# A Hyena filter and a cosine-gated MLP on one core: transformed data made the stationary operand of the last step, x turned in blocks by VectorE, and places of 129 elements

## The chip, the cores and the metric

The kernel runs on one core of a Trainium2 chip. The metric is the device time of one launch in microseconds. All arithmetic is float32. In the profile PE is TensorE's matmuls, PEld its weight loads, DVE is VectorE, ACT ScalarE, POOL GpSimd, SP SyncE, which issues every DMA of this kernel.

## What is computed

```python
# x, v: (4, 12480, 128); pos_emb: (12480, 64); w1: (64, 64); w2: (64, 128)
h_filt = (np.maximum(pos_emb @ w1, 0.0) @ w2) * np.exp(-0.01 * pos)[:, None]
u = x * v
L = 2 * S
y = np.fft.irfft(np.fft.rfft(u, n=L, axis=1) * np.fft.rfft(h_filt, n=L, axis=0)[None], n=L, axis=1)[:, :S]
a = (x * y).reshape(B * S, D)
# moe_w_in: (128, 2048), moe_w_out: (2048, 128)
h = a @ w_in
out = (h * np.cos(h)) @ w_out
```

A long causal convolution over 12,480 positions in each of 128 channels, multiplied by x, and then a feed-forward layer on each of the 49,920 rows. (The float64 weights of the second part are turned into float32 on the chip.)

## The kernel before

**The transform.** The convolution is a Fourier transform of length N1 x N2 = 96 x 120, done by matmuls in two steps each way. A sequence position is n1 x 120 + n2, with n1 up to R = 104. The steps of one batch, by the names of the functions that issue them:

- u: x and v are loaded with n1 on the partitions, multiplied (L395), and the sums and differences of positions that mirror each other are written to the big buffer `slots` (L401).
- f1 (`f1_mm`, L407): the transform over n1. For each channel a 104 x 124 slice of `slots` (n1 by place) is the stationary operand, loaded as weights, and the table c1 (192 columns) streams. `f1_evict` (L415 to L425) writes the result back over the same channel.
- f2 (`f2_mm`, L448): the transform over n2. A table w (124 x 120) is stationary, and all 128 channels of one place, real and imaginary, stream: 256 columns. `f2_product` (L467 to L474) multiplies by the filter's transform h, on DVE and POOL.
- i1 (`i1_mm`, L479): back over k2. For each channel a 120 x 96 slice of `slots` is stationary and the table cs (120 columns) streams. `i1_evict` (L487, L489) writes sums and differences.
- i2 (`i2_mm`, L504): back over k1. A table tm (96 x 104) is stationary and all channels of one place stream (128 columns). The output has n1 on the partitions; `i2_out` (L511) multiplies it by x, loaded the same way (xs), and stores a group of four n2 (`n2s`) to zd in HBM.

A float32 matmul appears in the profile as two instructions, each with its own weight load.

**The layout of slots.** It is `[P, CB, 2*N2, 2]`: 64 pairs of channels, then 240 places, then the two channels of the pair. A slice of one channel over the places steps by two elements; all channels of one place are 64 pairs, 480 elements apart. `parts`, `above`, `aT` and `ftile` are views or tiles of the same kind.

**The feed-forward part.** 98 tiles of up to 128 rows of four n2, so up to 512 columns. `moe_load` (L727) brings a tile zb from zd; `moe_turn` transposes it with four TensorE transposes (L126) into PSUM, and ACT copies it to `at` (L737). For each of 16 chunks of 128 hidden units: `moe_up` (L743, then ACT L746, DVE L749, POOL L752), `moe_act` (ACT L757, DVE L759) and, four steps later, `moe_down` (L768). `moe_back` transposes the result again with TensorE and `moe_store` writes it.

**The order.** It is written out by hand. First the setup: the filter's network, f1 of the filter, f1 of batch 0 (beside the conversion of the first weights), f2 of both together (`f2_both_units`, which keeps h in hd and w in wd), i1 of batch 0 (beside the conversion of the second weights and some tables). `cs` is loaded just before f2 of both, into a pool of its own. From then on the main loop goes through 98 x 16 steps of the feed-forward part and, between them, advances the convolution of the batches by generators: each yields how many steps its piece counts for (I1_STEPS 0.8 a channel pair, I2_STEPS 1.5 a group, and so on), and `owed` keeps the balance. `load(n)` first advances the convolution until the rows of tile n are made. A tile is loaded at step 12 of the tile two before it, and turned at step 3 of the tile before it. `units` gives each kind of piece its pattern: `before` (loads, some pieces ahead), `mm` (matmuls), `after` (what follows the matmuls, one piece late).

Of the kernel before, what the change touches and what calls it, by code (L numbers as in the profile page):

```python
# [30 lines left out]
def kernel(  # L31
# [74 lines left out]
    LAG = 4  # L106
    WCOL = 256

    dram = ctx.enter_context(tc.tile_pool(name="dram", bufs=1, space=DRAM))
    hd = dram.tile([N1 // 2, N2, 2, CB, 4], F32, name="hd")  # L110
    zd = dram.tile([NROWS, G, D], F32, name="zd")
# [241 lines left out]
    def filter_out(pool, bank, aT, slots, j, w2_sb):  # L353

        ps = bank()
        for i, jj in enumerate((j, H - 1 - j)):
            nc.tensor.matmul(ps[0:FR, i * 2 * D:(i + 1) * 2 * D], aT[:, jj, 0:FR],
                             w2_sb[:, :], start=True, stop=True)
        above = pool.tile([FR, 2, CB, 2], F32, name="above", bufs=2)
        pj = ps[0:FR, :].rearrange("p (n b i) -> p n b i", n=4, i=2)  # L360
        nc.scalar.copy(out=above[:, :, :, :], in_=pj[:, 2:4])
        a = H - 2 - 2 * j
        for place, op in ((a, ALU.add), (ODD + a, ALU.subtract)):
            nc.vector.tensor_tensor(
                slots[0:FR, :, place:place + 2, :].transpose([0, 2, 1, 3]),
                pj[:, 1::-1], above[:, :, :, :], op=op)
# [14 lines left out]
    def clear_gap(u):  # L381

        nc.gpsimd.memset(u[:, :, H:ODD, :], 0.0)
# [13 lines left out]
    def u_sums(u, tiles, a):  # L397
        both = tiles[0][:, :, :].rearrange("p h (n b i) -> p h n b i", n=UA, i=2)
        below, above = both[:, 0, ::-1, :, :], both[:, 1, :, :, :]
        for place, op, e in ((a, ALU.add, nc.gpsimd), (ODD + a, ALU.subtract, nc.vector)):  # L400
            e.tensor_tensor(u[0:R, :, place:place + UA, :].transpose([0, 2, 1, 3]),  # L401
                            below, above, op=op)


    def f1_mm(ps, u, b, i):

        nc.tensor.matmul(ps[0:KE, i * 2 * N1:(i + 1) * 2 * N1], u[:, b, 0:KE, i],  # L407
                         c1[0:u.shape[0], :, :].rearrange("p r k -> p (r k)"),
                         start=True, stop=True)
# [10 lines left out]
    def f1_evict(ps, b, share):  # L420
        copy, negated = f1_takers(b, share)
        pj = ps[:, 0:4 * N1].rearrange("p (i r k) -> p r k i", i=2, r=2)
        copy(out=parts[0:ODD, :, :, b, :], in_=pj[0:ODD])
        yield
        copy(out=parts[ODD:KE, 0, :, b, :], in_=pj[ODD:KE, 1])  # L425
        negated(parts[ODD:KE, 1, :, b, :], pj[ODD:KE, 0])
        yield

    def f1_evict_filter(ps, b, share):

        copy, negated = f1_takers(b, share)
        pj = ps[:, 0:4 * N1].rearrange("p (i k) -> p k i", i=2)
        near, far = ftile[:, b, :, :], above[:, b, :, :]
        copy(out=near[0:ODD], in_=pj[0:ODD, 0:N1 + KF])
        copy(out=far[0:ODD], in_=pj[0:ODD, N1 + KF:])
        yield
        copy(out=near[ODD:KE, 0:N1], in_=pj[ODD:KE, N1:])
        negated(near[ODD:KE, N1:], pj[ODD:KE, 0:KF])
        negated(far[ODD:KE], pj[ODD:KE, KF:N1])
        yield  # L440

    def f2_mm(ps, w, k1, i, filt=False):
# [3 lines left out]
        pi = ps[0:N2, :].rearrange("p (r b g i) -> p g r b i", r=2, g=2, i=2)[:, i]  # L446
        if not filt:
            nc.tensor.matmul(pi, w[:, i, :], parts[0:KE, :, k], start=True, stop=True)  # L448
        elif k < KF:
            both = ftile[0:KE, :, k:k + N1 + 1:N1, :].rearrange("p b r i -> p r b i")  # L450
            nc.tensor.matmul(pi, w[:, i, :], both, start=True, stop=True)
        else:
            for r, src in enumerate((ftile[0:KE, :, k, :], above[0:KE, :, k - KF, :])):
                nc.tensor.matmul(pi[:, r], w[:, i, :], src, start=True, stop=True)

    def f2_product(pool, ps, h, k1, whole):


        y = parts[0:N2, :, k1:k1 + 2, :, :].rearrange("p r k b i -> p r b (k i)")
        t = pool.tile([N2, 2, CB, 4], F32, name="t", bufs=1 + whole)  # L460
        uu = ps[0:N2, :].rearrange("p (r b j) -> p r b j", r=2, j=4)
# [15 lines left out]
    def i1_mm(ps, b, i):  # L477
        for r in range(2):
            nc.tensor.matmul(  # L479
                ps[0:N1, (i * 2 + r) * N2:(i * 2 + r + 1) * N2],  # L480
                parts[0:N2, r, :, b, i],
                cs[:, r, :], start=True, stop=True)

    def i1_evict(pool, ps, b):
# [3 lines left out]
        for h, op in ((0, ALU.add), (1, ALU.subtract)):  # L488
            nc.vector.tensor_tensor(slots[0:N1, b, h * N2:(h + 1) * N2, :], pj[:, 0],  # L489
                                    other[:, :, :], op=op)  # L490
            yield

    def i2_mm(ps, t, g, part):
        for i in range(part * G // 2, (part + 1) * G // 2):
# [8 lines left out]
            for r, place in enumerate(places):  # L503
                nc.tensor.matmul(ps[0:R, i * D:(i + 1) * D], t[:, i, r, :],  # L504
                                 slots[0:N1, :, place, :], start=(r == 0), stop=(r == 1))

    def i2_out(pool, ps, xs, b, g):
        if b == 0:
            yield
        zs = pool.tile([R, 2, UA, D], F32, name="zs")  # L510
        nc.vector.tensor_tensor(  # L511
            zs[:, :, :, :].rearrange("p h n d -> p (h n d)"), ps[0:R, :],
            xs[:, :, :].rearrange("p h n -> p (h n)"), op=ALU.mult)
        z = zs[:, :, :, :].rearrange("p h n d -> p (h n) d")
        row = (b * NG + g) * R
        if row > 0:
            nc.sync.dma_start(zd[row:row + R, :, :], z)
        else:
            zbs[0] = z
        made[0] += 1  # L520
        yield

    rows_psum = []
    made = [0]
    zbs = {}
# [65 lines left out]
    def f2_units(bank):  # L591
        with tc.tile_pool(name="there", bufs=3) as pool:
            ws, hs = {}, {}

            def before(j):
                ws[j] = pool.tile([KE, 2, N2], F32, name="w")
                nc.sync.dma_start(ws[j][:, :, :], wd[j, :, :, :])
                hs[j] = pool.tile([N2, 2, CB, 4], F32, name="h")
# [11 lines left out]
    def f2_both_units(bank):  # L610

        with tc.tile_pool(name="both", bufs=2) as pool:
# [15 lines left out]
            def after(j, ps):  # L628
                h = pool.tile([N2, 2, CB, 4], F32, name="h", bufs=3)
                nc.scalar.activation(h[:, :, :, :].rearrange("p r b j -> p (r b j)"),  # L630
# [34 lines left out]
    def i2_units(bank, b, bufs):  # L665

        with tc.tile_pool(name="back", bufs=2, side="left" if b else "right") as pool:
            ts, xss = {}, {}

            def before(j):  # L670
                ts[j] = pool.tile([N1, G, 2, R], F32, name="tm", bufs=bufs)
                xss[j] = pool.tile([R, 2, UA * D], F32, name="xs", bufs=bufs)
                load_pairs(xss[j], x, b, n2s(j)[0], n2s(j)[UA])
                if b == 0 and j not in SOME:
                    return make_group(pool, j, ts[j], 1)
                nc.sync.dma_start(ts[j][:, :, :, :], td[j, :, :, :, :])

            def mm(j, ps, i):
                if i == 0:
                    ps = bank()  # L680
                i2_mm(ps, ts[j], j, i)
# [3 lines left out]
                             lambda j, ps: i2_out(pool, ps, xss.pop(j), b, j),  # L685
                             4 if b == 0 else 2, ahead=bufs - 1, skip=int(b == 0))

    def inverse_units(bank, b):
# [6 lines left out]
        new = u_units(b + 1, 3, slots[0:R, :, :, :],  # L695
# [10 lines left out]
    def forward_units(bank, back):  # L706

        f2 = f2_units(bank)
        next(f2)
        yield from f1_units(bank, slots[0:R, :, :, :])  # L710
# [13 lines left out]
    def moe_load(pool, n):  # L724
        m, row = rows_of(n), first_row(n)
        zb = pool.tile([P, G, D], F32, name="zb", bufs=2)
        nc.sync.dma_start(zb[0:m, :, :], zd[row:row + m, :, :])  # L727
        zbs[n] = zb

    def moe_turn(pool, n):  # L730
        m = rows_of(n)
        zb = zbs.pop(n)
        pt = ps_h.tile([P, BANK], F32, name="ph")
        for i in range(G):
            transpose(pt[:, i * m:(i + 1) * m], zb[0:m, i, :], ident)
        at = pool.tile([D, BANK], F32, name="at")
        nc.scalar.copy(out=at[:, 0:G * m], in_=pt[:, 0:G * m])  # L737
# [62 lines left out]
    with tc.manual_schedule():  # L800
        with tc.tile_pool(name="psum", bufs=8, space=PSUM) as psum, \
# [5 lines left out]
            slots = spool.tile([P, CB, 2 * N2, 2], F32, name="slots")  # L807
            parts = slots[:, :, 0:2 * N1, :].rearrange("p b (r k) i -> p r k b i", r=2)
            above = slots[:, :, 2 * N1:2 * N2, :]
            aT = above.rearrange("p b j i -> p b (j i)")  # L810
# [5 lines left out]
            with tc.tile_pool(name="layers", bufs=1, side="right") as pool:  # L816
# [10 lines left out]
                first_u = u_units(0, 3, slots[0:R, :, :, :],  # L827
# [24 lines left out]
            ftile = fpool.tile([P, CB, N1 + KF, 2], F32, name="ftile")  # L852
            clear_gap(ftile[0:FR, :, :, :])
            with tc.tile_pool(name="out", bufs=1, side="right") as pool:
                for j in range(H // 2):
                    filter_out(pool, bank, aT, ftile, j, w2_sb)
                    for _ in range(1 + (j % 3 == 0)):
                        next(first_u)
            f1 = f1_units(bank, ftile[0:FR, :, :, :], 0.53, f1_evict_filter)
# [15 lines left out]

            def beside(units, pieces, more=lambda pool: iter(())):
                with tc.tile_pool(name="convert", bufs=1) as pool:
                    convert, other = convert_units(pool, pieces), more(pool)
                    for i, _ in enumerate(units):
                        if i % 14 == 0:  # L880
# [6 lines left out]
            beside(f1_units(bank, slots[0:R, :, :, :], 0.55),  # L887
                   [(wind[:, c], w) for c, w in in_pieces])
            lpool = ctx.enter_context(tc.tile_pool(name="late", bufs=1))
            cs = third_table(lpool)  # L890
            nc.sync.dma_start(cs[:, :, :], csd[:, :, :])
            for _ in f2_both_units(bank):
# [3 lines left out]
            wpool = ctx.enter_context(tc.tile_pool(name="weights", bufs=1))  # L896
            rows, tw_t = last_tables(wpool)
# [22 lines left out]
        mpool = ctx.enter_context(tc.tile_pool(name="moe", bufs=2))  # L920

# [4 lines left out]
        def convolutions():  # L926
            for b in range(B):
# [5 lines left out]
                if b + 1 < B:  # L933
                    yield from forward_units(bank, backs[b + 1])
# [11 lines left out]
        moe_turn(mpool, 0)  # L946
        steps = [(n, c) for n in range(NALL) for c in range(NFC)]
        hidden, gates, ots, obs = {}, {}, {}, {}
        for i in range(len(steps) + LAG):
            if i < len(steps):  # L950
                n, c = steps[i]
                if n == 0 and c == NFC // 2:
                    load(1)
                if c == NFC - 4 and n + 2 < NALL:
                    load(n + 2)
# [8 lines left out]
            if i < len(steps):  # L964

                if c == (LAG - 1 if n else NFC - 2) and n + 1 < NALL:
                    moe_turn(mpool, n + 1)
# [37 lines left out]
```

## Time and profile before

| what | value |
|---|---|
| time, three runs | 3759.83, 3760.59, 3761.09 us (median 3760.59) |
| span of the profiled execution | 3758.9 us, 47,177 instructions |
| setup, up to the first product of the feed-forward part | 343.9 us |
| f1 of batches 1, 2, 3 (first to last matmul) | 594 to 729, 1410 to 1541, 2233 to 2364 us |
| f2 of batches 1, 2, 3 | 734 to 1021, 1549 to 1835, 2371 to 2658 us |
| i1 of batches 1, 2, 3 | 1031 to 1172, 1843 to 1986, 2665 to 2809 us |
| i2 of batches 0 to 3 | 338 to 565, 1178 to 1383, 1992 to 2206, 2815 to 2946 us |
| feed-forward part alone | 2946 us to the end |
| DMA | 209,499 packets, 276.14 MB, 73 GB/s on average |

The time of a run is that of the launch; the profiled execution is known by its span, which starts with its first instruction and ends with its last. In a group of instructions the columns are line, engine, operation, tiles, shape and number; busy time and mean duration of one in ns; and the engine's idle time before them with what ended it. A matmul's duration is longer than its share of the stream, since matmuls are pipelined: the distance from start to start is what counts.

### The profile page before, as it was taken

The page shows a single profiled execution, that of the slowest core. Times are in us where ns is not written, and L with a number is a line of the kernel's source. Part 1 is how long each engine was busy: PE and PEld are TensorE (multiplying, and loading weights), DVE is VectorE, ACT ScalarE, POOL GpSimd, SP SyncE. Part 2 cuts the span into 40 slices and gives each one's busy share as a digit, 9 for nine tenths or more (in the row PEclk, how much of TensorE's full clock was granted, in tenths as well). Part 3 has the DMA queues.
Part 4 walks back from the last instruction along what each step waited for, and adds up shares of the span by engine and source line. Part 5 has one row for each costly group of instructions (what it writes and reads, how often), then busy time and mean ns, then how long its engine had stood idle before and what let it go on. Part 6 is the DMA issues. An engine that isn't in the chain of part 4 may idle for free.

```text
span 3758.9 us, 47177 instructions
## 1 busy us (share of the span) xinstructions
PE 3690.6 (98%) x13546; PEld 2110.4 (56%) x13546; DVE 2773.7 (74%) x5586; ACT 2508.2 (67%) x4660; POOL 2557.6 (68%) x2318
## 2 busy tenths in 40 slices
PE   7898999999999999999999999999999999999999
PEld 6777555555566556555565556555566544444444
DVE  8887997687866787788766776788765666666666
ACT  5757776766665557766665567666664677777777
POOL 6666776588845665688745664788644677777776
PEclk9999999999999999999999999999999999999999
DMA  6263551022203650122104530122105200000000
GB/s 167 64 185 107 155 167 33 25 72 79 72 12 91 181 151 12 40 79 77 52 18 128 180 105 21 52 79 76 38 21 172 76 23 17 17 23 18 17 23 13
DMA packets 209499, 276.14 MB, mean 73 GB/s; under 512 B 17111, under 2 KB 146535, under 8 KB 209111
## 3 DMA queue, kind: packets, MB, share of 16 engines
q1 hardware_dynamic: 209239, 273.12, 24.8%
q8 instruction: 109, 1.79, 0.2%
q14 instruction: 151, 1.24, 0.1%
HBM read 193.64 MB, written 79.42 MB: 73 GB/s over the span
## 4 chain that ended last, share of the span: by engine, by line
PE 88%; DVE 3%; POOL 3%; ACT 2%; DMA 2%; issue 1%; SPq 0%; POOLq 0%; DVEq 0%; ACTq 0%
PE ph L743 33%; PE acc L768 28%; PE cv L504 5%; PE cv L768 5%; PE cv L479 4%; PE cv L407 3%; PE cv L448 3%; PE ph L126 2%; POOL f L752 1%; PE ps L407 1%; PE ps L448 1%; DMA tm<-td 1%; DMA wd<-w 1%; ACT cs L757 1%; DVE k L749 1%
## 5 line engine op out<-in xcount | busy, mean ns | idle before, releaser
L752 POOL TENSOR_TENSOR f<-a,k 128x512 f32<-128x512 f32 (+1 forms) x1568 | 1986.2, 1267 | 1060.5 <-DVE k L749 1059.1
L743 PE MATMUL ph<-at,w_in_sb 128*128 128x512 f32 (+1 forms) x3136 | 1599.0, 591 | 3.7 <-DVE gt L759 2.7
L746 ACT ACTIVATE a<-ph,quarter 128x512 f32<-128x512 f32 (+1 forms) x1568 | 1071.2, 683 | 704.8 <-PE ph L743 695.2
L768 PE MATMUL acc<-gt,w_out_sb 128*128 128x512 f32 (+1 forms) x2688 | 1370.3, 591 | 0.0
L759 DVE TENSOR_TENSOR gt<-ph,cs 128x512 f32<-128x512 f32 (+1 forms) x1568 | 1077.3, 687 | 359.9 <-ACT cs L757 341.8
L757 ACT ACTIVATE cs<-f 128x512 f32<-128x512 f32 (+1 forms) x1568 | 981.0, 626 | 366.6 <-POOL f L752 364.3
L749 DVE TENSOR_SCALAR k<-a 128x512 f32<-128x512 f32 (+1 forms) x1568 | 792.9, 506 | 550.7 <-ACT a L746 524.2
L768 PEld LDWEIGHTS acc<-gt,w_out_sb 128*128 128x128 f32 x2688 | 508.4, 189 | 642.8 <-issue 631.9
L743 PEld LDWEIGHTS ph<-at,w_in_sb 128*128 128x128 f32 x3136 | 553.2, 190 | 337.7 <-issue 257.5
L474 POOL TENSOR_TENSOR slots<-slots,t 120x256 f32<-120x256 f32 x384 | 312.9, 821 | 59.9 <-DVE t L467 25.6
L504 PEld LDWEIGHTS cv<-slots,tm 96*104 96x104 f32 x1920 | 238.6, 169 | 106.8 <-issue 85.4
L504 PE MATMUL cv<-slots,tm 96*104 96x128 f32 x1920 | 251.7, 273 | 9.9 <-POOL tm L297 5.0
L768 PE MATMUL cv<-gt,w_out_sb 128*128 128x512 f32 (+1 forms) x448 | 224.5, 583 | 1.0 <-DVE gt L759 1.0
L479 PEld LDWEIGHTS cv<-cs,slots 120*96 120x96 f32 x1536 | 176.7, 167 | 67.2 <-issue 65.2
L479 PE MATMUL cv<-cs,slots 120*96 120x120 f32 x1536 | 183.2, 266 | 0.0
L448 PEld LDWEIGHTS cv<-slots,w 124*120 124x120 f32 x576 | 103.7, 184 | 124.3 <-issue 112.3
L407 PEld LDWEIGHTS cv<-c,slots 104*124 104x124 f32 x768 | 132.6, 192 | 72.2 <-issue 60.0
L448 PE MATMUL cv<-slots,w 124*120 124x256 f32 x576 | 173.0, 380 | 0.0
L407 PE MATMUL cv<-c,slots 104*124 104x192 f32 x768 | 151.8, 327 | 5.4 <-DVE gt L759 3.5
L768 PEld LDWEIGHTS cv<-gt,w_out_sb 128*128 128x128 f32 x448 | 84.9, 190 | 104.8 <-issue 99.5
L489 DVE TENSOR_TENSOR slots<-cv,other 96x240 f32<-96x240 f32 x384 | 133.1, 394 | 1.5 <-ACT other L487 1.4
L395 DVE TENSOR_TENSOR xt<-xt,vt 104x256 f32<-104x256 f32 x177 | 132.6, 751 | 0.6 <-DMA vt<-in_v_dram 0.6
(131 smaller groups left out, 2520.9 us busy)
## 6 DMA issues: line engine op xcount, KB each, us to landing
h<-hd SPq DMA_DIRECT2D x144, 240.0 KB
tm<-td SPq DMA_DIRECT2D x96, 312.0 KB
xt<-in_x_dram SPq DMA_DIRECT2D x120, 208.0 KB
vt<-in_v_dram SPq DMA_DIRECT2D x120, 208.0 KB
xs<-in_x_dram SPq DMA_DIRECT2D x120, 208.0 KB
zd<-zs SPq DMA_DIRECT2D x119, 208.0 KB
zb<-zd SPq DMA_DIRECT2D x96, 256.0 KB
w<-wd SPq DMA_DIRECT2D x144, 116.2 KB
```

The lines of the kernel that those rows point to most:

```text
L407: nc.tensor.matmul(ps[0:KE, i * 2 * N1:(i + 1) * 2 * N1], u[:, b, 0:KE, i], c1[0:u.shape[0], :, :].rearrange("p r k -> p (r k)"), start=Tr ...
L448: nc.tensor.matmul(pi, w[:, i, :], parts[0:KE, :, k], start=True, stop=True)
L474: nc.gpsimd.tensor_tensor(y[:, r], y[:, r], t[:, r], op=op)
L479: nc.tensor.matmul(ps[0:N1, (i * 2 + r) * N2:(i * 2 + r + 1) * N2], parts[0:N2, r, :, b, i], cs[:, r, :], start=True, stop=True)
L504: nc.tensor.matmul(ps[0:R, i * D:(i + 1) * D], t[:, i, r, :], slots[0:N1, :, place, :], start=(r == 0), stop=(r == 1))
L743: nc.tensor.matmul(ph[:, 0:m], w_in_sb[:, c * P:(c + 1) * P], ats[n][:, 0:m], start=True, stop=True)
L746: nc.scalar.activation(a[:, 0:m], ph[:, 0:m], AF.Identity, bias=quarter[:, 0:1], scale=INV_TWO_PI)
L749: nc.vector.tensor_scalar(out=k[:, 0:m], in0=a[:, 0:m], scalar1=ROUND, scalar2=ROUND, op0=ALU.add, op1=ALU.subtract)
L752: nc.gpsimd.tensor_tensor(f[:, 0:m], a[:, 0:m], k[:, 0:m], op=ALU.subtract)
L757: nc.scalar.activation(cs[:, 0:m], f[:, 0:m], AF.Sin, scale=TWO_PI)
L759: nc.vector.tensor_tensor(gt[:, 0:m], ph[:, 0:m], cs[:, 0:m], op=ALU.mult)
L768: nc.tensor.matmul(accs[n][:, 0:m], w_out_sb[:, c, :], gt[:, 0:m], start=(c == 0), stop=(c == NFC - 1))
```

## The change

- `slots` becomes `[P, 2*N2, 129]`: a place is 129 elements, 128 channels in a row and one unused. All channels of one place are now contiguous; a slice of one channel steps by 129 elements (516 bytes). `parts`, `above`, `ftile` and hd follow. `filter_out` takes two unused stretches of `slots` for its temporary.
- In i2 the operands change places: the 128 channels of one place are loaded as weights and the table's 104 columns stream. The output has the channels on the partitions and n1 in the columns, as the feed-forward part needs it.
- `moe_turn` is gone: `moe_load` loads `at` from zd, which now has the channels first, in two or three pieces of up to 104 rows. A tile is loaded at step 8 of the tile before it. The first tile is made in `at` itself.
- x must now be turned for the multiplication. For each batch, 64 DMAs copy x from HBM to HBM into blocks (`blocks_units`); they are issued during f1, one every second piece, for batch 0 during its f1 and f2. For each group four DMAs load 32 partitions each (`blocks_load`), and VectorE transposes 32 x 32 blocks (`blocks_turn`) right after the product of the group before.
- `cs` is loaded after f2 of both, with the other tables.

```diff
-    zd = dram.tile([NROWS, G, D], F32, name="zd")
+    xd = dram.tile([B, H, D // SQ, UA, ROWB, NB, SQ], F32, name="xd")
+    zd = dram.tile([B * NG, D, G, R], F32, name="zd")
...
-        nc.tensor.matmul(ps[0:KE, i * 2 * N1:(i + 1) * 2 * N1], u[:, b, 0:KE, i],
+        nc.tensor.matmul(ps[0:KE, i * 2 * N1:(i + 1) * 2 * N1], u[:, 0:KE, 2 * b + i],
...
-                parts[0:N2, r, :, b, i],
+                parts[0:N2, r, :, 2 * b + i],
                 cs[:, r, :], start=True, stop=True)
...
-                nc.tensor.matmul(ps[0:R, i * D:(i + 1) * D], t[:, i, r, :],
-                                 slots[0:N1, :, place, :], start=(r == 0), stop=(r == 1))
+                nc.tensor.matmul(ps[0:D, i * R:(i + 1) * R], slots[0:N1, place, 0:D],
+                                 t[:, i, r, :], start=(r == 0), stop=(r == 1))
+
+    def blocks_units(b):
+        for a in range(D // SQ):
+            for i in range(UA):
+                for r in range(ROWB):
+                    start = x[b, r * N2 + i, a * SQ:(a + 1) * SQ]
+                    nc.sync.dma_start(
+                        xd[b, :, a, i, r, :, :],
+                        bass.AP(tensor=start.tensor, offset=start.offset,
+                                ap=[[UA * D, H], [ROWB * N2 * D, NB], [1, SQ]]))
+                    yield
+
+    def blocks_load(t, b, g):
+        first, _, second, _ = n2s(g)
+        for a in range(D // SQ):
+            start = xd[b, first // UA, a, 0, 0, 0, :]
+            nc.sync.dma_start(
+                t[a * SQ:(a + 1) * SQ, :, :],
+                bass.AP(tensor=start.tensor, offset=start.offset,
+                        ap=[[(second - first) // UA * (D // SQ) * UA * ROWB * NB * SQ, 2],
+                            [NB * SQ, UA * ROWB], [1, NB * SQ]]))
+
+    def blocks_turn(pool, t):
+        xt = pool.tile([D, G, R], F32, name="xt", bufs=2)
+        nc.vector.transpose(
+            xt[:, :, :].rearrange("d i (n r) -> d n i r", r=ROWB),
+            t[:, :, :].rearrange("p n (i r) -> p n i r", r=ROWB))
+        return xt
...
-        zb = pool.tile([P, G, D], F32, name="zb", bufs=2)
-        nc.sync.dma_start(zb[0:m, :, :], zd[row:row + m, :, :])
...
+            nc.sync.dma_start(to[:, :, done:done + rows], zd[group, :, :, n1:n1 + rows])
...
-            slots = spool.tile([P, CB, 2 * N2, 2], F32, name="slots")
-            parts = slots[:, :, 0:2 * N1, :].rearrange("p b (r k) i -> p r k b i", r=2)
+            slots = spool.tile([P, 2 * N2, DP], F32, name="slots")
+            parts = slots[:, 0:2 * N1, 0:D].rearrange("p (r k) d -> p r k d", r=2)
```

(SQ is 32, ROWB 8, NB 13, DP 129.)

## The prediction

> **What bounds the kernel now.** I read the page's busy times first, then the chain of waits, then the stage windows.
>
> ```profile
> PE 3690.6 (98%) x13546; PEld 2110.4 (56%) x13546; DVE 2773.7 (74%) x5586; ACT 2508.2 (67%) x4660; POOL 2557.6 (68%) x2318
> PEclk9999999999999999999999999999999999999999
> PE 88%; DVE 3%; POOL 3%; ACT 2%; DMA 2%; issue 1%; SPq 0%; POOLq 0%; DVEq 0%; ACTq 0%
> ```
>
> TensorE is busy 98% of the span at full clock and holds 88% of the chain. The windows of the stages (columns: length; busy time of PE, PEld, DVE, ACT, POOL; clock; DMA share; GB/s) show where it is not:
>
> ```profile
> 64.00:115.00 51.00, 48.49 (x259) 45.92 (x260) 48.02 (x156) 36.94 (x162) 42.91 (x78) 0.92 0.33 97
> 115.00:167.00 52.00, 44.46 (x255) 43.23 (x253) 43.40 (x123) 41.21 (x124) 33.88 (x43) 0.93 0.23 64
> 167.00:270.00 103.00, 95.88 (x480) 74.56 (x480) 85.56 (x193) 57.66 (x155) 65.51 (x93) 0.98 0.57 167
> 270.00:335.00 65.00, 56.03 (x512) 54.58 (x512) 48.42 (x149) 40.48 (x125) 46.32 (x61) 0.97 0.29 88
> 594.00:727.00 133.00, 132.62 (x481) 82.77 (x482) 93.18 (x198) 96.36 (x204) 67.07 (x54) 0.99 0.07 21
> 1030.00:1180.00 150.00, 150.00 (x776) 97.58 (x775) 101.44 (x238) 90.52 (x183) 70.66 (x56) 1.00 0.07 20
> ```
>
> The first four are setup: f1 of the filter, f1 of batch 0, f2 of both, i1 of batch 0; TensorE has only 2.5, 7.5, 7 and 9 us idle in them. The last two, f1 and i1 of batch 1 beside the last step's products, have none. So what counts is the time of each matmul, which is the longer of its stream and of the next weight load (PEld overlaps PE, one load ahead). Groups by shape:
>
> ```profile
> L504 PEld LDWEIGHTS cv<-slots,tm 96*104 96x104 f32 x1920 | 238.6, 169 | 106.8 <-issue 85.4 <-POOL tm L297 5.2 <-PE acc L768 5.1
> L479 PEld LDWEIGHTS cv<-cs,slots 120*96 120x96 f32 x1536 | 176.7, 167 | 67.2 <-issue 65.2 <-PE ph L743 1.9
> L407 PEld LDWEIGHTS cv<-c,slots 104*124 104x124 f32 x768 | 132.6, 192 | 72.2 <-issue 60.0 <-POOL slots L401 6.0 <-PE ph L743 3.8
> L448 PE MATMUL cv<-slots,w 124*120 124x256 f32 x576 | 173.0, 380 | 0.0
> L126 PE MATMUL ph<-ident,zb 128*128 128x128 f32 x384 | 57.7, 273 | 0.0
> ```
>
> And the timeline, where n matmuls in a row give (time - one duration)/(n-1) from start to start:
>
> ```profile
> 1042.00 1.40 PE L479 MATMUL cv<-cs,slots 120*96 120x120 f32 x12
> 603.73 1.14 PE L407 MATMUL cv<-c,slots 104*124 104x192 f32 x6
> 1203.26 1.05 PE L504 MATMUL cv<-slots,tm 96*104 96x128 f32 x8
> 600.92 0.60 PE L126 MATMUL ph<-ident,zb 128*128 128x128 f32 x4
> ```
>
> That is (1.40-0.266)/11 = 103 ns for i1 (120 columns), (1.14-0.327)/5 = 163 ns for f1 (192), (1.05-0.273)/7 = 111 ns for i2 (128), (0.60-0.273)/3 = 109 ns for a transpose (128). A column costs 0.83 ns (592 ns at 512 columns, 273 at 128: 319/384). Loads have the same slope, 163 ns at 96 contiguous columns (L357) and 190 at 128: 27/32 = 0.84, so about 83 ns of a load is fixed latency and the rest occupies the path: 80 ns for i1's 96 columns, 103 for f1's 124. Both lie under their stream today, i1's with 22 ns to spare, f1's with 60.
>
> **The change, part by part.** *Removed: the turn of each tile* (L126 from zb, 388 instructions): 388 x 109 ns = -42 us. Its ACT copies (96 x 574 ns) leave ACT, which bounds nothing; the load waits that they end ("ACT at L737", 17 us on PEld) lie under running matmuls.
>
> *i2 with the data stationary* (1920 instructions): the stream falls from 128 to 104 columns, 87+2 = 89 ns, but the load grows from 104 to 128 columns, 190-83 = 107 ns. The longer sets the pace: 107 to 109 against 111 gives -4 us. If the load were free, -22 ns x 1920 = -42 us. I take -4, since load and stream show one slope.
>
> *f1 and i1 with stationary places 516 bytes apart* (before 8 bytes). No row has such a read. Below: 0.83 ns a column as now, nothing added. Above: the rows nearest to a jump per element are the streams that jump once per pair, i2's moving read (64 jumps of 1,920 bytes in 111 ns, 1.73 ns a jump) and the loads with a step of 8 bytes, counted per pair of columns: (167-83)/48 = 1.75 and (192-83)/62 = 1.76 ns. No plain read in the trace takes a pair faster than that, and all of these are 2 to 6 ns slower than contiguous ones (111 against 109; 192 against 83+103 = 186), as a limit just reached would show. If a lone element costs what a pair does, a place is 1.70 ns, and I take that: 124 places 211 ns against a 163 ns stream (+48), 96 places 163 ns against 103 (+60). One load of each burst still lies under a 512-column matmul; the timeline shows bursts of 4 to 6 for f1 and 8 to 12 for i1, so 4/5 and 9/10 pay. Beside the products: 768 x 4/5 x 48 = +29 and 1536 x 9/10 x 60 = +83 us. In setup, 512 f1 x 48 = 25 less the idle 10 us, of which I count half: +20; 512 i1 x 60 = 31 less half of 9: +26. Sum +158, or 0 at the lower end.
>
> The Trainium skill (Advanced Engine Details and Errata, Memory Cachelines) speaks against the change: SBUF is read in lines of 16 bytes, and it takes two hits on a line to hide the access, while a new line for each access is penalised. It gives no size; the sum by it has the sign of the upper end, and the present 8-byte step, two hits a line, is the last that would be free.
>
> *f2 with contiguous rows*: (220-216) x 768 = -3 us at most. I take -2.
>
> *Writes of pairs 516 bytes apart* by DVE and ACT (f1 and i1 evictions): L364 already writes pairs with a jump and takes 410 ns for 256, L473 contiguous 412. Nothing added; a quarter more would be 100 ns x 1000 on DVE, which has 26% idle. POOL's L474 and L401 lose their jumps and can only gain.
>
> *x by blocks*: 64 DMAs per batch of 60 x 13 = 780 runs of 128 bytes, HBM to HBM, 49,920 in all or 3,120 per engine of 16. In the trace's packet records a 256-byte packet takes 18 ns and a 1,024-byte one 46; the mean over queue q1 is 0.248 x 16 x 3758.9/209,239 = 71 ns. So 56 to 222 us of every engine per batch. Forward f1 has 133 us with the queue 7% busy, 124 free: hidden below 40 ns a packet. I take 25 (78 us), nearer to the short packets. In setup half of them (39 us) meet f2 of both, 57% x 103 = 59 us busy: 98 of 103, and there ACT already waits 36.5 us for the hd stores (three buffers). I add +8 us (0 to +65).
>
> *Loads of x*: four DMAs of 32 rows x 1,664 bytes replace one of 208; the tile's load and the zd store change shape, with half a tile (8 steps of 1.7 us or more) ahead of use. SP has more to issue, at 0.24 to 0.39 us each, 480 + 256 + some 120 more against 120 less: +0.25 ms of a queue that mostly waits; behind a late issue stand tm, w, h and the next tile. In the last i2, 131 us for 30 groups (4.4 us each, DMA 53%), a group's 4 x 32 rows are 128 packets of about 90 ns (71 x 1664/1305): 0.7 us if spread over 16 engines, 5.8 us if on two. I take +5 (0 to +40).
>
> The Trainium skill (DMA: Bandwidth & Descriptors, Why a DMA increments its semaphore by 16 and not by 1) says that a DMA uses the largest number of engines up to 16 that divides both sides' slowest dimension: here 32 and 2, hence 2. By it the last i2 would be late by (5.8-4.4) x 30 = 42 us instead of 5.
>
> *DVE*: 120 block transposes of 416 columns, not shown; below L759's 586 ns for 416, above twice that. The products shrink from 680 to 586. With 590, 30 x 0.5 = +15 us of DVE in batch 0's i2, where it has 232 of 259 us: hidden, but PE's slack is 8, so +3 (0 to +15). *cs* is loaded after f2 of both rather than before it: a load lands in some 3 us, under the last products' POOL chain (4.1 us for six): +3 (0 to +3).
>
> Sum: -42 -4 +158 -2 +8 +5 +3 +3 = +129, 3758.9 + 129 = 3888 us of span. The three runs' median, 3760.6, lies 1.7 above the span: 3890.
>
> **The rivals.** *The loads keep their pace* (0.83 ns a column at any step). For: transposes load 128 columns in 141 ns instead of 190, so the path can deliver twice what plain fp32 loads ask, which leaves room for a new line each column. Against: the 2 to 6 ns that pairs cost. Then -42-4-2+19 = -29: 3731 us; with i2's load free 3693. It holds in full below 1.07 ns a place in i1 (103/96); from about 1.25 ns, where i1 pays 17 ns on 1,382 loads beside the products (23 us) and some 6 us in setup, the 29 us are gone and the other side begins.
>
> *The 128-byte transfers back up.* Beyond 40 ns a packet, f1 cannot carry them, and f2's w and h loads queue behind. At 71 ns: 222-124 = 98 us per batch, three times, and about 65 in setup: +360 on either case, 4,090 or 4,250. For: nothing so short crosses HBM now. Against: the short packets recorded are quick.
>
> **How the numbers follow.** Places priced by the line 0.55, pace kept 0.34, back-up 0.11. The likeliest has its own range 3840 to 3950 (1.55 to 1.9 ns, DMA terms at their ends). Down to 3690 the range takes in the second case; what it leaves out is the back-up and the far ends. A change under 0.2% (7.5 us) cannot be told from none: 0.03, out of the edges of the first two. Faster 0.33, slower 0.64.
>
> **What would show it.** PEld of L407 and L479 at 83 + 124 x 1.7 = 294 ns and 83 + 163 = 246 ns, and start-to-start 211 and 163 in the timeline, the windows of f1 and i1 longer by 10 and 28 us per batch; i2 near 108; no L126 from zb. Loads still at 192 and 167 make the forecast wrong at its main term; waits on w, h or xb show the DMA terms wrong.

## The result and the profile after

The changed kernel takes 4029.8 us (median of 4, 4025.41 to 4032.33) against 3760.84 us: a ratio of 1.0716, 95% interval 1.07 to 1.0731. It is slower by 269 us, above the forecast of 3890 and above 3950, where the range of its likeliest case ended. The span of the profiled execution is 4023.4 us.

The page of the changed kernel, busy times, clock, and the chain of waits by engine and by line:

```profile
PE 3879.8 (96%) x13154; PEld 2312.3 (57%) x13154; DVE 2794.2 (69%) x5706; ACT 2507.8 (62%) x4562; POOL 2530.2 (63%) x2318
PEclk9999999999999999999999999999999999999999
PE 78%; DMA 17%; DVE 2%; POOL 1%; issue 1%; ACT 1%; SPq 1%; DVEq 0%; POOLq 0%; ACTq 0%
PE ph L797 28%; PE acc L822 23%; DMA xb<-xd 7%; PE cv L484 6%; DMA tm<-td 6%; PE cv L822 5%; PE cv L411 4%; PE cv L453 3%; PE ps L411 3%; PE ps L484 2%; PE cv L509 2%; DMA wd<-w 2%; PE ph L132 1%; DMA zd<-zs 1%; POOL f L806 1%
```

Two things happened. TensorE is busy for 189 us longer, though it has 392 instructions less. And DMA, 2% of the chain before, holds 17%, with the loads of x's blocks (xb) and of the tables (tm) at its head. The groups by shape (line, engine, operation, tiles, shape, number; busy time, mean ns; idle time before and its cause) show the first:

```profile
L484 PEld LDWEIGHTS cv<-cs,slots 120*96 120x96 f32 x1536 | 289.8, 266 | 59.1 <-issue 58.4 <-PE ph L797 0.7
L411 PEld LDWEIGHTS cv<-c,slots 104*124 104x124 f32 x768 | 195.3, 312 | 57.2 <-issue 28.3 <-PE ph L797 5.8 <-POOL slots L406 3.3
L509 PEld LDWEIGHTS cv<-tm,slots 96*128 96x128 f32 x1920 | 253.9, 199 | 204.4 <-issue 93.0 <-DMA tm<-td 37.4 <-PE acc L822 27.9
L509 PE MATMUL cv<-tm,slots 96*128 96x104 f32 x1920 | 262.2, 283 | 80.6 <-DMA tm<-td 74.1 <-POOL tm L303 1.9 <-DVE xt L538 1.9
```

i1's weight load (L484, before L479) took 167 ns and takes 266; f1's (L411, before L407) 192 and now 312. The median distance between the starts of successive matmuls, from the trace's records, went from 102 to 174 ns in i1 and from 162 to 223 in f1: 174/96 = 1.81 and 223/124 = 1.80 ns a place. In i2 (L509) it is 112 ns after 111, and TensorE waits there for tm.

The windows of i2 of batches 1 and 3 (columns: length; busy PE, PEld, DVE, ACT, POOL; clock; DMA share; GB/s), in the kernel before:

```profile
1178.00:1383.00 205.00, 203.35 (x854) 119.42 (x853) 156.72 (x278) 113.04 (x185) 130.33 (x111) 1.00 0.59 177
2815.00:2946.00 131.00, 131.00 (x677) 87.65 (x676) 67.50 (x119) 57.73 (x97) 57.19 (x45) 1.00 0.56 168
```

and in the changed one:

```profile
1284.00:1522.00 238.00, 215.41 (x853) 122.73 (x852) 167.43 (x315) 115.77 (x188) 130.75 (x116) 0.99 0.52 150
3056.00:3231.00 175.00, 147.75 (x668) 93.62 (x667) 78.54 (x149) 58.35 (x95) 57.21 (x46) 0.92 0.40 127
```

TensorE, busy for all but 2 us of these windows before, idles 23 and 27 us, and in the last one its clock was granted at 0.92; yet the DMA engines are on average less busy than before (0.40 for 0.56). That would fit transfers that use a few of the 16 engines; the third experiment tests it. The chain of waits in 40 us of the last window (start, length, what), with the first line its shares (a wait that reaches over the edge of the 40 us counts whole, so they add up to more than 100%):

```profile
by line: DMA xb<-xd 70.8%; DMA zd<-zs 18.7%; DMA tm<-td 17.5%; SPq L529 3.2%; DVE k L803 2.3%; issue 2.0%; DVE gt L813 1.5%; DVE xt L538 1.3%; PE cv L509 0.8%; DVE zs L549 0.2%; DVEq L549 0.1%; DVEq L538 0.1%; DVEq L813 0.1%; DVEq L803 0.1%
...
3092.57 7.66 DMA xb<-xd
...
3100.25 6.62 DMA xb<-xd
3106.88 6.75 DMA xb<-xd
...
3113.65 7.50 DMA zd<-zs
...
3132.62 7.00 DMA tm<-td
```

Each transfer there takes about 7 us, tm and zd too, although these two are as large as before. Stage by stage (first to last matmul, us):

| stage | before | after |
|---|---|---|
| f1 of the filter and of batch 0 | 102 | 116 |
| f2 of both | 98 | 115 |
| i1 of batch 0 | 60 | 90 |
| i2 of batches 0, 1, 2, 3 | 227, 206, 214, 131 | 238, 238, 236, 175 |
| f1 of batches 1, 2, 3 | 135, 131, 131 | 144, 144, 144 |
| f2 of batches 1, 2, 3 | 286, 287, 286 | 283, 283, 282 |
| i1 of batches 1, 2, 3 | 142, 144, 144 | 174, 174, 173 |
| feed-forward part alone | 808 | 788 |

### The profile page after: what moved, and what is told of

Read it like the earlier page. It is cut to its first block, busy times and chain, and to the rows that moved or that the text cites. A ratio compares the mean times of both kernels' runs of the same rounds, so it can differ in the third digit from the quotient of the medians.

```text
span 4023.4 us, 47439 instructions
## 1 busy us (share of the span) xinstructions
PE 3879.8 (96%) x13154; PEld 2312.3 (57%) x13154; DVE 2794.2 (69%) x5706; ACT 2507.8 (62%) x4562; POOL 2530.2 (63%) x2318
## 4 chain that ended last, share of the span: by engine, by line
PE 78%; DMA 17%; DVE 2%; POOL 1%; issue 1%; ACT 1%; SPq 1%; DVEq 0%; POOLq 0%; ACTq 0%
PE ph L797 28%; PE acc L822 23%; DMA xb<-xd 7%; PE cv L484 6%; DMA tm<-td 6%; PE cv L822 5%; PE cv L411 4%; PE cv L453 3%; PE ps L411 3%; PE ps L484 2%; PE cv L509 2%; DMA wd<-w 2%; PE ph L132 1%; DMA zd<-zs 1%; POOL f L806 1%
## 5 line engine op out<-in xcount | busy, mean ns | idle before, releaser
L803 DVE TENSOR_SCALAR k<-a 128x512 f32<-128x512 f32 (+1 forms) x1568 | 769.1, 491 | 650.0 <-ACT a L800 631.6
L509 PEld LDWEIGHTS cv<-tm,slots 96*128 96x128 f32 x1920 | 253.9, 199 | 204.4 <-issue 93.0
L479 POOL TENSOR_TENSOR slots<-slots,t 120x256 f32<-120x256 f32 x384 | 289.2, 759 | 85.2 <-DVE t L472 48.3
L509 PE MATMUL cv<-tm,slots 96*128 96x104 f32 x1920 | 262.2, 283 | 80.6 <-DMA tm<-td 74.1
L484 PEld LDWEIGHTS cv<-cs,slots 120*96 120x96 f32 x1536 | 289.8, 266 | 59.1 <-issue 58.4
L484 PE MATMUL cv<-cs,slots 120*96 120x120 f32 x1536 | 282.1, 331 | 0.0
L411 PEld LDWEIGHTS cv<-c,slots 104*124 104x124 f32 x768 | 195.3, 312 | 57.2 <-issue 28.3
L411 PE MATMUL cv<-c,slots 104*124 104x192 f32 x768 | 189.8, 377 | 1.9 <-DVE gt L813 1.9
L494 DVE TENSOR_TENSOR slots<-cv,other 96x240 f32<-96x240 f32 x384 | 141.2, 416 | 3.3 <-ACT other L492 1.3
L549 DVE TENSOR_TENSOR zs<-cv,xt 128x416 f32<-128x416 f32 x119 | 69.2, 581 | 81.3 <-DMA zd<-zs 73.3
```

The lines of the kernel that those rows point to most:

```text
L479: nc.gpsimd.tensor_tensor(y[:, r], y[:, r], t[:, r], op=op)
L484: nc.tensor.matmul(ps[0:N1, (i * 2 + r) * N2:(i * 2 + r + 1) * N2], parts[0:N2, r, :, 2 * b + i], cs[:, r, :], start=True, stop=True)
L509: nc.tensor.matmul(ps[0:D, i * R:(i + 1) * R], slots[0:N1, place, 0:D], t[:, i, r, :], start=(r == 0), stop=(r == 1))
L803: nc.vector.tensor_scalar(out=k[:, 0:m], in0=a[:, 0:m], scalar1=ROUND, scalar2=ROUND, op0=ALU.add, op1=ALU.subtract)
```

## The experiments

The theory after the result had two parts: strided weight loads cost some 170 us, and loads of xb that run on two DMA engines cost some 110. The rivals: the losses come from the short copies of x through HBM, from the number of DMA issues, or from the pitch of 129.

### The price of a place, by itself

A kernel of its own, which leaves the whole computation out: 40 float32 matmuls for each step of the stationary read, one after another.

```diff
+        for _ in range(40):
+            nc.tensor.matmul(ps[0:96, 0:32], big[:, 0:12384:129], narrow[:, :], start=True, stop=True)
```

> The kernel leaves the whole computation out: it is 80 matmul instructions (40 float32 matmuls) of 96 stationary columns and 32 moving ones for each step of the stationary read (1, 2, 3, 4, 5, 8, 32, 120, 128, 129, 130, 132 elements), then the same with a moving read of 96 columns at steps 1, 2, 4, 129. Theory (a price per line of 16 bytes touched): loads of 96 columns pace at some 80 ns from start to start at steps 1 and 2, 130 at step 3 and 170 to 175 from step 4 on, the same at 120, 128, 129 and 132; moving reads 82 at steps 1 and 2, 170 to 175 at 4 and 129. Rival (a conflict of banks that depends on the pitch): 128 differs from 129 and 130, and small steps such as 5 stay near 80.

With 32 streamed columns the clock fell to half in the middle of step 1 (0.68 on average). From there on steps 1 to 3 came out at one value, 160 ns: the expected 80 and 130 could not be seen, and only the steps from 4 on (163 to 183 ns) could be read. So it was repeated with 96 streamed columns.

> As micro_steps, the computation left out, but each matmul streams 96 columns, so that the clock should stay up; the stationary steps are 1, 2, 3, 4, 5, 8, 6, 120, 128, 129, 130, 132. Theory (a place in a new 16 bytes costs about 1.7 to 1.9 ns whatever the pitch, and closer ones follow the clock): start to start 82 ns at steps 1 and 2, 163 to 183 from step 4 on, step 3 between. Rival (the cost grows with the distance): step 4 well below step 129.

The clock stayed at 0.996. The timeline of TensorE (start, length of 80 instructions): L34 is step 1, then 2, 3, 4, 5, 8, 6, 120, 128, 129, 130 and 132 at L56; L58 to L64 are the moving reads at steps 1, 2, 4 and 129.

```profile
47.47 7.04 PE L34 MATMUL ps<-flat,big 128*96 128x96 f32 x80
54.34 7.28 PE L36 MATMUL ps<-flat,big 128*96 128x96 f32 x80
61.45 10.65 PE L38 MATMUL ps<-flat,big 128*96 128x96 f32 x80
71.94 14.30 PE L40 MATMUL ps<-flat,big 128*96 128x96 f32 x80
...
127.40 14.26 PE L48 MATMUL ps<-flat,big 128*96 128x96 f32 x80
141.50 13.32 PE L50 MATMUL ps<-flat,big 128*96 128x96 f32 x80
154.65 14.03 PE L52 MATMUL ps<-flat,big 128*96 128x96 f32 x80
...
204.04 7.09 PE L60 MATMUL ps<-big,narrow 128*32 128x96 f32 x80
210.98 13.92 PE L62 MATMUL ps<-big,narrow 128*32 128x96 f32 x80
224.72 14.05 PE L64 MATMUL ps<-big,narrow 128*32 128x96 f32 x80
```

From the start of one line to the next, over 80: 86, 89, 131, then 177 ns at step 4, 176 at 120, 164 at 128 and 173 at 129. The cost does not grow with the distance: it doubles between 2 and 4 elements, with step 3 between, and from there on stays between 164 and 183 ns for every step tried. A price per 16 bytes touched fits: 96 reads at step 3 touch 72 pieces of 16 bytes and at step 2 they touch 48, which at 177/96 = 1.84 ns is 132 and 88 ns, against 131 and 89 measured. This is what the Trainium skill's rule (Advanced Engine Details and Errata, Memory Cachelines) describes, lines of 16 bytes and two hits to hide one. The run gives it a size, 1.7 to 1.9 ns for a float32 that is alone in its line against 0.9 for one of a contiguous read. The steps from 4 on took the same time in the first measurement, at half the clock (step 5 167 ns in both, step 129 173), so this price did not follow TensorE's clock. A moving read pays the same (172 and 173 ns). And 129 is no better than 128; what makes the 10% between the longer steps was not looked for.

### The layout alone

The kernel before with the new layout only (and, since it needs the room, `cs` loaded after f2 of both):

```diff
-        nc.tensor.matmul(ps[0:KE, i * 2 * N1:(i + 1) * 2 * N1], u[:, b, 0:KE, i],
+        nc.tensor.matmul(ps[0:KE, i * 2 * N1:(i + 1) * 2 * N1], u[:, 0:KE, 2 * b + i],
...
-            slots = spool.tile([P, CB, 2 * N2, 2], F32, name="slots")
+            slots = spool.tile([P, 2 * N2, DP], F32, name="slots")
```

> The kernel before with places of 129 elements alone (data still streams in i2, each tile is turned by TensorE, x is loaded as before; cs is loaded after f2 of both, since the room is needed). Theory (the weight loads of f1 and i1 are most of the loss): f1 and i1 start to start 223 and 174 ns, setup +40 us, f1 and i1 of batches 1 to 3 +135 us, in all 3925 to 3940 us. Rival (the loss is in the new transfers and the swap): under 3800 us.

3935.94 us, ratio 1.0462 (1.0446 to 1.0479): +175 us. Its stages are those of the changed kernel where f1 and i1 run (116 and 90 us in setup, 144 to 147 and 175 to 177 later) and those of the kernel before in i2 (227, 206, 215, 130) and in f2 of both (98). So the layout by itself costs about two thirds of the loss, and i2's loss is not the layout's.

### The order of rows in xb's loads

```diff
-                        ap=[[(second - first) // UA * (D // SQ) * UA * ROWB * NB * SQ, 2],
-                            [NB * SQ, UA * ROWB], [1, NB * SQ]]))
+                        ap=[[NB * SQ, UA * ROWB],
+                            [(second - first) // UA * (D // SQ) * UA * ROWB * NB * SQ, 2],
+                            [1, NB * SQ]]))
...
-            xt[:, :, :].rearrange("d i (n r) -> d n i r", r=ROWB),
-            t[:, :, :].rearrange("p n (i r) -> p n i r", r=ROWB))
+            xt[:, :, :].rearrange("d (h i) (n r) -> d n i r h", h=2, r=ROWB),
+            t[:, :, :].rearrange("p n (i r h) -> p n i r h", h=2, r=ROWB))
```

> The changed kernel with one edit: the rows of each load of xb in another order (16 rows outermost and the two halves inside), so that the slowest dimension is 16 and not 2; the same four DMAs, bytes and runs, and VectorE's transpose writes its columns accordingly. Theory (two DMA engines carry these loads, 64 runs of 1,664 bytes each at 69 ns = 4.4 us a group, and tm and zd wait behind them): i2 of batches 1 to 3 falls from 238, 236 and 175 us to about 205, 210 and 135, in all 4030 to 3915 to 3930 us. Rival (the number of issues on SP, or the short pieces of zd, make i2 late): no change, 4020 to 4035 us.

3925.14 us, ratio 1.0433 (1.0416 to 1.0449): 105 us less than the changed kernel. The windows of i2 of batches 1 and 3:

```profile
1287.00:1494.00 207.00, 207.00 (x852) 122.28 (x851) 167.93 (x315) 115.57 (x188) 130.52 (x115) 1.00 0.63 172
2999.00:3132.00 133.00, 132.07 (x673) 88.64 (x672) 88.89 (x149) 57.49 (x96) 57.29 (x46) 1.00 0.60 168
```

TensorE is full again, with the same four DMAs a group, the same bytes, the same runs of 1,664 bytes and about the same 0.59 us of SP for each. Only the slowest dimension of the source differs, 16 for 2. The number of issues and the short pieces in which the tiles come from zd are thereby out as the cause. The trace does not name a packet's engine, but its packet records tell two engines from sixteen. The queue's line of the page (packets, MB, share of 16 engines), first of the changed kernel, then of x_order:

```profile
q1 hardware_dynamic: 502089, 298.70, 27.9%
q1 hardware_dynamic: 508809, 298.73, 29.8%
```

These are 6,720 packets more, all of 4 bytes: 14 for each of the 480 loads. And in the last i2 of the changed kernel exactly two packets were in flight for 46% of the time, in that of x_order for 3%. The time fits as well: 64 runs x 69 ns, six of tm at 131 ns and eight of zd at 69 make 5.8 us on each of the two, and the last i2 took 175/30 = 5.8 us a group. The i2 of batches 1, 2 and 3 became 31, 29 and 44 us shorter, which is the whole of the 105; that of batch 0 stayed at 238.

### The copies of x

> x_order without the block copies of batches 1 to 3 (their 192 DMAs of 780 runs of 128 bytes; x of these batches is not copied, and batch 0's blocks are read in their place). Theory (the copies are hidden under f1: 13 ns a run): within 5 us of x_order. Rival (they delay f1, the tiles of the feed-forward part or f2): more than 15 us faster than x_order.

```diff
-        f2, back, blocks = f2_units(bank), backs[b], blocks_units(b)
+        f2, back, blocks = f2_units(bank), backs[b], iter(())
...
-            start = xd[b, first // UA, a, 0, 0, 0, :]
+            start = xd[0, first // UA, a, 0, 0, 0, :]
```

3925.72 us against 3925.14: nothing. 192 DMAs of 780 runs of 128 bytes, from HBM to HBM, are hidden under f1; each run took 13 ns in the packet records. The rival of the back-up falls.

> x_order with the 64 block copies of batch 0 moved ahead: one every third piece of f1 of the filter and of f1 of batch 0, so that none is left for f2 of both. Theory (the copies share the DMA engines with the hd and wd stores in f2 of both, which took 115 us instead of 98): f2 of both about 98 us, in all 12 to 18 us less than x_order. Rival (the slower stage comes from the new layout or the stores themselves): no change.

```diff
+                blocks = blocks_units(0)
                 for i, _ in enumerate(f1):
+                    if i % 3 == 0:
+                        next(blocks, None)
...
-                        if i % 4 == 0:
+                        if i % 3 == 0:
                             next(blocks, None)
```

3905.88 us: 19 less, one more than expected. f2 of both, first with the copies beside it (x_order):

```profile
183.00:298.00 115.00, 94.39 (x480) 72.75 (x478) 82.98 (x188) 52.63 (x138) 59.81 (x91) 1.00 0.70 173
```

and without them (x_order_setup):

```profile
182.00:280.00 98.00, 95.58 (x480) 74.52 (x480) 83.84 (x190) 52.74 (x139) 60.11 (x92) 0.98 0.59 173
```

The same 480 matmuls in 98 instead of 115 us, at the same 173 GB/s. The shares of the chain of waits in these two windows, first with the copies, then without:

```profile
by line: DMA wd<-w 61.7%; PE ps L453 13.5%; DVE w L299 10.8%; issue 4.4%; DMA hd<-h 3.8%; PE ps L455 3.8%; PE ps L459 2.7%; DVE slots L472 0.9%; DVEq L299 0.8%; ACT h L670 0.5%; DVE t L472 0.4%; ACTq L670 0.0%; SPq L672 0.0%
by line: PE ps L453 46.1%; PE ps L455 19.4%; PE ps L459 16.1%; DMA wd<-w 11.0%; DVE w L299 4.1%; DMA hd<-h 3.8%; issue 1.6%; ACT h L670 0.6%; DVEq L299 0.2%; SPq L672 0.1%
```

Without the copies TensorE holds 82% of the chain; with them the stores of w to wd hold 62%. VectorE, which makes the next w (L299), waits 26.2 us for these stores with the copies and 5.3 us without, and TensorE's weight loads wait 32.6 and 13.8 us for it.

### The pitch, and where the loads fall

> x_order with places of 128 elements instead of 129. Theory (the first measurement by itself gave 163 ns for 96 places at a step of 128 and 173 at 129): f1 and i1 start to start fall by 6 to 10%, i1 from 174 to about 164, in all 3925 to 3900 to 3912 us. Rival (a pitch that is a power of two collides): slower than x_order.

One line, `DP = D`. 3902.87 us: 22 less than with 129, as the single measurement said (164 against 173 ns for 96 places). In the kernel below, which has the same places, i1 goes from 174 to 164 ns from start to start. The unused element of each place does harm; why 128 reads faster than 129 stays open.

> x_order with the convolution's pieces issued in two halves of a step, after moe_up's matmul and after moe_down's, rather than all after both. Theory (a load under a 512-column matmul is free, and two of some ten loads of i1 and two of five of f1 are then covered instead of one): 15 to 25 us less than x_order. Rival (loads are pulled ahead only within a run of equal shapes, or the shorter runs cost elsewhere): no change or slower.

```diff
                 hidden[i] = moe_up(mpool, n, c)
+            owed += 0.5
+            while owed > 0.0:
+                owed -= next(conv, owed)
...
-            owed += 1.0
+            owed += 0.5
```

3908.83 us: 16 less. f1 of batches 1 to 3 takes 141, 139 and 139 us instead of 145, 143 and 144, i1 171 instead of 174: as one more load of each step under a matmul of 512 columns would give.

> x_order with the three edits together: places of 128 elements, batch 0's block copies ahead of f2 of both, and the pieces in two halves of a step. Theory (three separate costs, 22, 19 and 16 us measured alone): they add up, less a little where the second half of a step already covers what the cheaper place saves: 3865 to 3876 us, still slower than the kernel before, since some 140 us of the loads' cost remain. Rival (one cost under three names): 3890 us or more.

3867.7 us, ratio 1.0285 (1.0267 to 1.0304). The three costs add up (22 + 19 + 16 = 57, measured 57). i1's and f1's loads:

```profile
L484 PEld LDWEIGHTS cv<-cs,slots 120*96 120x96 f32 x1536 | 299.4, 252 | 125.7 <-issue 109.6 <-ACT a L801 8.6 <-ACT cs L812 3.6
L411 PEld LDWEIGHTS cv<-c,slots 104*124 104x124 f32 x768 | 208.5, 292 | 117.1 <-issue 50.9 <-PE cv L411 18.2 <-POOL slots L406 3.5
```

252 and 292 ns are still far above the 167 and 192 of the kernel before, and no version here is faster than that kernel. Whether the data can be i2's weights in the old layout of pairs was not tried.

## Why the prediction was right and wrong, step by step

The sign and the main mechanism were right; the time was not, because one term of the sum, the loads of x, was mis-sized by a factor of twenty (+5 for +105). Of the 269 us, the layout alone gives +175, the order of rows +105 and batch 0's copies +19; the remaining -30 are what is left of the gain from the turn (forecast -42, not measured alone) after what the new work adds elsewhere, 11 us in batch 0's i2 among it. (The sum takes the layout's effect from the kernel before and the others from the changed one.)

- **The strided loads**, +158 forecast at 1.70 ns a place: 1.81 and 1.80 in place, and the layout alone costs 175, with a wait of some 6 us for the later tables inside and about 1 us gained in f2. The mechanism held, as did the choice of the upper bound, read from the streams that jump per pair; the size was off by a tenth. The loads were forecast at 294 and 246 ns and took 312 and 266.
- **The loads of x**, +5 (0 to +40): this step failed. The two prices were there, 0.7 us a group if spread over 16 engines and 5.8 us if on two, and the sum took nearly the first without a row that spoke for it. The runs showed two engines, and 105 us. That the 5.8 came out to the tenth of a microsecond is luck: the prediction had 64 runs of xb alone at 90 ns, a mean over all packets, where they took 69 ns (4.4 us) and tm and zd in the same two engines made up the rest. The range went wrong as well: it reached to about the 42 us worked out for the last i2 and left out the other batches, whose groups take some 7 us. There the chain of waits also holds loads of at and of the next batch's x of 7 to 8 us each, and every i2 was late: by 32, 22 and 44 us in batches 1 to 3. The rule of the Trainium skill (DMA: Bandwidth & Descriptors, Why a DMA increments its semaphore by 16 and not by 1) agrees with the runs: two engines for the loads with 2 outermost, and 15 packets of 4 bytes for each of the 192 copies with 60 outermost (2,880 fewer in x_order_one_batch). The measured price of an outermost 2 is 105 us.
- **The copies of x**, 25 ns a run taken: 13 measured, and hidden beside f1, so the back-up was no danger. But in f2 of both they cost 19 us and not 8: the sum looked at ACT's wait for the hd stores, but what the copies delayed on TensorE's path were the stores of w.
- **i2 with the data stationary**, -4: 112 ns after 111, no gain. A stream of 104 columns would give 89 ns and the load of 128 columns 107, by the prediction's own rows, so the load is the nearer limit; the 42 us of a free load were rightly not counted on.
- **The turn removed**, -42: L126 from zb is gone. It was not measured alone. The feed-forward part alone became 20 us shorter; 112 transposes fewer at 109 ns are 12 of them, and the rest is that 20 matmuls of 512 columns fewer (427 ns each) are left for it.
- **Writes of pairs**, 0: they did become slower, ACT's L428 (before L423) from 467 to 585 ns for 384 elements and DVE's L494 (before L489) from 394 to 416. ACT and DVE had room (62% and 69% busy); what this cost the end was not measured alone.
- **cs and DVE**, +3 each: TensorE waits 6.4 us for cs; the transposes take 601 ns each, and i2 of batch 0, with the fullest VectorE, became 11 us longer. It is 238 us with the rows of xb's loads in either order and 227 with the layout alone, so it belongs neither to that order nor to the layout; what part of it is the transposes' was not separated.

## What to carry to other kernels

Where an operand of TensorE is read with a step of four float32 or more, count twice the time per column (1.7 to 1.9 ns for 0.9 here), and see whether a stream of the next instruction's length covers it: an operand swap that makes one step's reads contiguous must be charged with the strided reads that it gives the others. Look at the outermost dimension of both sides of each DMA before its bytes; a small one can make a load of 208 KB hold back everything that shares its engines, while the average DMA share falls. A bound of the range that is worked out for one stage should be worked out for every stage that issues the same transfers.

## What was not expected of the hardware

- Matmuls with 96-column loads and 32-column streams, issued without a gap, did not keep the clock up: it was granted at half from step 1 of the first measurement (0.68 on average over the whole) until the streams there had 96 columns, and at 0.996 where all had 96.
- 207,360 packets of 128 bytes, most of them from HBM to HBM, took 13 ns each, where 256 bytes took 18 ns and 1,024 bytes 46: per byte over twice the price of 1,024, yet half of the 25 ns that the prediction took, and hidden under f1.
- VectorE's block transpose of 416 columns took 601 ns where it writes runs of eight, and 886 ns in x_order, where neighbouring elements are written 832 bytes apart.
